# Three places instead of four in a weight ring, and a second part of a key cache kept on chip

## The chip, the cores and the metric

The kernel runs on one core of a Trainium2 chip. The core has five engines with a queue of instructions each: TensorE (PE in the profile, its weight loads PEld), VectorE (DVE), ScalarE (ACT), GpSimd (POOL) and the sync engine (SP), which here only issues DMA transfers. Sixteen DMA engines move data between HBM and SBUF, the on-chip memory of 128 partitions; matmuls write to PSUM. The metric is the device time of one execution in microseconds.

## The reference

Two sequences of one token each, width 576, run through two layers; each is an attention over a cache and a gated MLP, and both layers read the same weights and the same caches:

```python
x = A_x                                     # [2, 1, 576]
for layer in range(2):
    x = x + A(layernorm(x)); x = x + B(layernorm(x))

def A(x):                                   # 32 heads of 128, 8192 cached positions
    q = (x @ wq)                            # wq [576, 4096]
    p = softmax(einsum("bhqd,bhkd->bhqk", q, k_cache) * 128 ** -0.5)
    return einsum("bhqk,bhkd->bhqd", p, v_cache) @ wo      # wo [4096, 576]

def B(x):
    return (gelu(x @ w_gate) * (x @ w_up)) @ w_down        # inner width 4608
```

The caches are [2, 32, 8192, 128] in float32, 268 MB for the keys and as much for the values. Reading both twice is most of the work.

## The kernel before

**Items.** Each layer's attention goes through 34 items. Items 0 to 29 are pairs of heads of one sequence, whose keys are eight parts of 1024 KB (`PART`, 128 partitions x 2048 floats). Items 30 to 33 (`SINGLE[0]` to `SINGLE[3]`) are single heads, with four parts each. Layer 0 takes the items in order, layer 1 backwards, so that what layer 0 used last is used first in layer 1 and can stay on chip: the keys of items 32 and 33 (`KEYS_HELD`) and the values of items 31, 32 and 33 (`VALUES_HELD`). Of the keys of item 31, the fourth part is kept as well, copied by ScalarE into a tile of PSUM (`kept`, line 636) and copied back in layer 1 (line 679).

**An item.** VectorE multiplies a part by the query (line 644; where an item's keys stay, into one of two product buffers instead of in place), GpSimd adds the two halves (line 661), and VectorE sums the rest to the scores (line 664, `add_up`). In the first items of layer 1, GpSimd (line 648) and ScalarE (line 654) take over some rows. Then the softmax on ScalarE (lines 713 and 721), and TensorE multiplies by the values (line 762). `add_up` frees the part of the keys, `values` the part of the values.

**The arena.** One tile, `space`, holds caches and weights. Its addresses are given out while the program is written: 6 slots of four parts from address 0, and a ring of places of 2304 floats (`PLACE`, 1152 KB over all partitions) from `RING` = 5 slots on, so that the sixth slot (slot 5) and the ring share their space. With four places, the arena has 50,176 floats. Each transfer is a function in one list, `queue`, and `pump` runs the head of the list as soon as its space is free; `done(key)` frees a space and pumps. So transfers are issued on the sync queue strictly in the order of the list, and a transfer whose space is taken holds up all behind it. The wait on the chip is for the last instruction that used the space.

**The ring's users, in the order of the list.** While the held items fill the slots, all other traffic goes through the ring: at the end of attention 0 two places are taken by the product buffers (`products`, line 279: places 2 and 3) and the eight groups of wo begin in the others. The list reads: keys of item 33, values of items 31 and 32, two groups of wo, two parts of the values of item 33 (into a slot), two groups of wo, two more parts of these values, four groups of wo. Each group is one use of the ring (line 296). Then the MLP of layer 0: 18 pieces of w_gate and w_up in two halves, most as two transfers (lines 248 and 258), and nine of w_down (line 271). Then nine pieces of wq for layer 1 (lines 227 and 238), and, as the last users, parts 0, 1 and 2 of the keys of item 31 and part 0 of item 30's (line 165). All later parts go into slots that held items leave. Slot 5 is next used by the first half of the keys of item 28, when the ring's last users are through. From item 27 on the kernel is back to pairs of slots. The rest of the weights, for the end of layer 1, are put wherever there is room in the whole arena (`fit`, line 107).

**Consumers of the ring.** wo is multiplied in line 812, w_gate and w_up in line 951, w_down in line 1004, wq in line 549. Between layer parts stand a norm and, in the MLP, the activation, both short chains over VectorE, TensorE, GpSimd and ScalarE. Small matmuls without use (line 526) stand between the pieces.

Of the kernel before, what the change touches and what calls it, by code (L numbers as in the profile page):

```python
# [36 lines left out]
PART = JC * DH  # L37
SLOT = 4 * PART
NSLOT = 6
PLACE = DF // 2  # L40
NPLACE = 4
RING = 5 * SLOT
END = RING + NPLACE * PLACE
HELD = 5


# [17 lines left out]
SINGLE = range(PAIRS, N)  # L64
# [3 lines left out]
class Arena:  # L68
# [32 lines left out]
    def ring(self, key, n):  # L101

        at = self.take(key, RING + self.turn % NPLACE * PLACE, n)
        self.turn += at is not None
        return at

    def fit(self, key, n, lo=0):

        for at in [self.at, lo] + sorted(end for _, end in self.live.values()):
            if lo <= at and at + n <= END and self.take(key, at, n) is not None:  # L110
                self.at = at + n
# [11 lines left out]
def decode_layers(ctx, tc, x_in, kc, vc, wq, wo, wg, wu, wd, out):  # L123
    nc = tc.nc
# [7 lines left out]

    space = consts.tile([P, END], F32, name="space")

# [10 lines left out]
    arena = Arena()  # L145
    queue, ready, places = [], {}, {}
# [9 lines left out]
    def part_at(at, n):  # L156
        return space[:, at:at + n]

    def part(at):
        return part_at(at, PART).rearrange("p (j d) -> p j d", d=DH)  # L160
# [6 lines left out]
    def cache(key, src, n, slots=None, pieces=None):  # L167

        parts = ITEMS[n].parts

        def make():
            at = arena.pair(key) if slots is None else arena.slots(key, slots, parts)
            if at is None:
                return False
            lo = 0
            for m in pieces or (parts,):
                load(at[lo], n, src, lo, lo + m)
                lo += m
            ready[key] = dict(enumerate(map(part, at)))
            places[key] = at  # L180
            return True

        queue.append(make)

    def half(key, src, n, k, slot):

        def make():
            at = arena.slots(key, (slot,), 4, k)
            if at is None:
                return False  # L190
            load(at[0], n, src, k, k + 4)
            ready.setdefault(key, {}).update((k + i, part(a)) for i, a in enumerate(at))
            return True

        queue.append(make)

    def one(key, src, n, k, where):

        def make():
            at = arena.ring((key, k), PART) if where is None else arena.take((key, k), places[where[0]][where[1]], PART)  # L200
            if at is None:
                return False
            load(at, n, src, k, k + 1)
            ready.setdefault(key, {})[k] = part(at)
            return True

        queue.append(make)
# [13 lines left out]
    def half_rows(key, w, us, first):  # L221

        width = w.shape[1] // 2
        rows = w.rearrange("r (s w) -> (r s) w", w=width).rearrange("(p u) w -> p u w", p=P)

        def transfers(t):
            nc.sync.dma_start(t.rearrange("p (u w) -> p u w", w=width), rows[:, us[0]:us[-1] + 1, :])

        weights(key, len(us) * width, first, transfers)

    def of_half(h, k):

        width = wq.shape[1] // 2
        rows = wq.rearrange("r (s w) -> (r s) w", w=width).rearrange("(p u) w -> p u w", p=P)

        def transfers(t):
            for e in range(2):
                nc.sync.dma_start(t[e::2, :], rows[e::2, 2 * k + (h + e) % 2, :])

        weights(("wq", 1, h, k), width, None, transfers)  # L240
# [38 lines left out]
    def products():  # L279

        def make():
            at = [RING + k * PLACE for k in (2, 3)]
            if not all(arena.clear(a, PLACE) for a in at):
                return False
            ready["products"] = [part(arena.take(("products", k), at[k], PART)) for k in range(2)]
            return True

        queue.append(make)

    def out_rows(layer, g):  # L290

        rows = wo[g * GH * DH:(g + 1) * GH * DH, :].rearrange("(p i) c -> p (i c)", i=GH)
        cut = 3 * D if layer == 0 and g == groups(layer)[-1] else GH * D

        def transfers(t):
            nc.sync.dma_start(t[:, :cut], rows[:, :cut])
            if cut < GH * D:
                nc.sync.dma_start(t[:, cut:], rows[:, cut:])

        weights(("wo", layer, g), GH * D, whole_at[layer], transfers)  # L300
# [16 lines left out]
    def groups(layer):  # L317
        return range(H // GH)[::1 - 2 * layer]

    def name(kind, layer, n):  # L320

        return kind, 1 if n in (KEYS_HELD if kind == "k" else VALUES_HELD) else layer, n

    def plan_first():
# [6 lines left out]
        for us in three:  # L331
            half_rows(("wq", 0, us[0]), wq, us, END - NU * H * DH // 2)
        last = PAIRS - 1
# [28 lines left out]
    def plan_second():  # L362

        for k in range(4):
            of_half(1, k)
        half_rows(("wq", 1, NU - 1), wq, single[-1], None)
        for k in range(4):
            of_half(0, k)
        last = PAIRS - 1
        k63, v63, k62, v62 = ("k", 1, SINGLE[3]), ("v", 1, SINGLE[3]), ("k", 1, SINGLE[2]), ("v", 1, SINGLE[2])  # L370

        for k in range(3):
            one(("k", 1, SINGLE[1]), kc, SINGLE[1], k, None)
        for k in range(4):
            one(("k", 1, SINGLE[0]), kc, SINGLE[0], k, (k63, k - 1) if k else None)

        one(("k", 1, last), kc, last, 0, (k63, 3))
        turns = iter(range(1, 5)), iter(range(4))
        for kind in "vvvvkkkk":
            if kind == "k":  # L380
                k = next(turns[0])
                one(("k", 1, last), kc, last, k, (k62, k - 1))
            else:
                k = next(turns[1])
                one(("v", 1, SINGLE[0]), vc, SINGLE[0], k, (v63, k))
        for k in range(5, 8):
            one(("k", 1, last), kc, last, k, (v62, k - 5))
        half(("k", 1, last - 1), kc, last - 1, 0, 5)
        half(("k", 1, last - 1), kc, last - 1, 4, 4)
        half(("v", 1, last), vc, last, 0, 0)  # L390
        half(("v", 1, last), vc, last, 4, 1)
        for n in range(last - 2, -1, -1):
            cache(("k", 1, n), kc, n)
            cache(("v", 1, n + 1), vc, n + 1)
        cache(("v", 1, 0), vc, 0, None, (4, 2, 1, 1))
        for g in groups(1):
            out_rows(1, g)
# [16 lines left out]
    plan_first()  # L414
    plan_mlp(0)
    plan_second()
    plan_mlp(1)
    pump()
# [59 lines left out]
    kept = psum1.tile([P, JC, DH], F32, name="kept")  # L478
# [62 lines left out]
    def attention(layer):  # L541
# [55 lines left out]
        def waited(n):  # L597

            return layer == 1 and n in seq[:5]
# [21 lines left out]
        def keys(n, k, m):  # L621

            key = name("k", layer, n)
            if m == 1:
                return ready[key][k]
            return part_at(arena.live[key, k][0], m * PART).rearrange("p (j d) -> p j d", d=DH)
# [3 lines left out]
        def multiply(n, k, m):  # L630

            if k == 0:
                S[n] = work.tile([P, SK * 2 // P], F32, name="S")
            u = t = keys(n, k, m)
            if n == SINGLE[1] and k == 3 and layer == 0:
                nc.scalar.copy(kept, t)
            if layer == 0 and n in KEYS_HELD:
                u = ready["products"][k % 2]
            every = m * JC
            rows = 12 if waited(n) else every  # L640
            q = qs[:, n % 2, :]
            if rows < JC and k == 0:
                nc.scalar.copy(q, qb[n])
            nc.vector.tensor_tensor(  # L644
                out=u[:, :rows, :], in0=t[:, :rows, :], in1=qb[n].unsqueeze(1).to_broadcast([P, rows, DH]), op=ALU.mult
            )
            if rows < JC:
                nc.gpsimd.tensor_tensor(
                    out=u[:, rows:, :], in0=t[:, rows:, :], in1=q.unsqueeze(1).to_broadcast([P, JC - rows, DH]),
                    op=ALU.mult,  # L650
                )
            r = own_rows(n, k, m)
            for j in range(r, every):
                nc.scalar.activation(  # L654
                    u[:, j, :], u[:, j, :], AF.Copy, accum_out=S[n][:, k * JC + j:k * JC + j + 1]
                )
            if at_once(n, k):
                prod[n, k] = u[:, :r, :]
                return
            half = prod[n, k] = u[:, :r, :DH // 2]  # L660
            nc.gpsimd.tensor_tensor(out=half, in0=half, in1=u[:, :r, DH // 2:], op=ALU.add)  # L661
# [230 lines left out]
        n, p = seq[-1], seq[-2]  # L892
# [154 lines left out]
```

## Time and profile before

| | |
|---|---|
| median of 3 runs | 2686.63 us (2686.57 to 2686.77) |
| profiled execution | 2686.79 us, span from first to last instruction 2685.0 us |
| bytes moved | 1154.30 MB, mean 430 GB/s |
| VectorE busy | 1806.0 us (67%) |
| GpSimd busy | 1161.8 us (43%) |
| TensorE busy | 914.4 us (34%) |
| ScalarE busy | 163.7 us (6%) |

A line of the instructions in order of time has the start in us, the time in us, the engine, the line of the kernel, the operation, output <- input, the shape and the number of instructions merged, and in brackets the idle time of the engine before it and what ended that. SPq is the sync queue, where the time runs from the first issue of a merged group to the last. A table of stretches has the stretch, its length, the busy time of PE, PEld, DVE, ACT and POOL with the number of instructions, the granted clock of TensorE, the mean busy share of the 16 DMA engines (packets are counted where they start, so a short stretch can be over 1) and GB/s. In a list of waits, a line has the waiting engine, what it waited for, the total in us, how often, and the longest. In the list of queues, a line has the packets, the megabytes and the share of 16 engines' time.

### The profile page before, as it was taken

What the parts mean: (1) busy time and instruction counts of PE and PEld (TensorE: products, weight loads), DVE (VectorE), ACT (ScalarE), POOL (GpSimd) and SP (SyncE); (2) the same over time, 40 slices, a digit from 0 to 9 for tenths busy, and PEclk for the clock granted to TensorE, in tenths of its full rate; (3) what the DMA queues carried; (4) which work ended last, traced back from release to release, by engine and by line L of the source; (5) the groups of instructions that cost most, each with busy time, mean ns of one, the idle gap of its engine ahead of it and who ended that gap; (6) DMA issues with size and microseconds to landing.
All of it is one profiled execution on the core that took longest, in us unless ns stands there. A gap on an engine that the chain in (4) does not pass through costs nothing. (4 is left out here: it accounts for less than half of the span.)

```text
span 2685.0 us, 17174 instructions
## 1 busy us (share of the span) xinstructions
PE 914.4 (34%) x7150; PEld 305.4 (11%) x7150; DVE 1806.0 (67%) x874; ACT 163.7 (6%) x786; POOL 1161.8 (43%) x261
## 2 busy tenths in 40 slices
PE   1323332332233233334663333233223323332356
PEld 0100010010001000111221101001000100010022
DVE  4876687677667766867037877667766776776640
ACT  0000000000000000000026000000000000000000
POOL 2543454354445444544028455445444543454420
PEclk7656666665666566566986665666566656656678
DMA  9999999999999999999999999999999999999998
GB/s 422 436 436 426 437 432 434 433 434 432 433 431 435 436 428 433 436 428 425 414 418 434 431 431 436 431 434 434 437 428 434 434 435 431 431 434 435 433 421 375
DMA packets 33950, 1154.30 MB, mean 430 GB/s; under 512 B 4152, under 2 KB 4176, under 8 KB 5968
## 3 DMA queue, kind: packets, MB, share of 16 engines
q1 hardware_dynamic: 33832, 1153.19, 99.8%
q8 instruction: 56, 0.92, 0.1%
q14 instruction: 22, 0.18, 0.0%
q10 hardware_dynamic: 40, 0.01, 0.0%
HBM read 1153.18 MB, written 0.00 MB: 429 GB/s over the span
## 5 line engine op out<-in xcount | busy, mean ns | idle before, releaser
L661 POOL TENSOR_TENSOR space<-space 128x3072 f32<-128x3072 f32 (+3 forms) x221 | 1128.6, 5107 | 1263.3 <-DVE space L644 1202.5
L644 DVE TENSOR_TENSOR space<-space,bank 128x6144 f32<-128x6144 f32 (+3 forms) x223 | 1112.7, 4991 | 560.2 <-DMA space<-in_A_k_cache_dram 496.8
L762 PE MATMUL acc<-space,prz 128*8 128x512 f32 x4096 | 594.6, 744 | 199.4 <-DMA space<-in_A_v_cache_dram 195.5
L664 DVE TENSOR_REDUCE S<-space 128x48 f32<-128x3072 f32 (+3 forms) x223 | 569.3, 2553 | 89.9 <-POOL space L661 89.6
L592 PE MATMUL bank<-qsb,pick 4*64 4x128 f32 (+1 forms) x256 | 46.3, 436 | 863.1 <-DVE space L644 853.1
L762 PEld LDWEIGHTS acc<-space,prz 128*8 128x8 f32 x4096 | 119.1, 104 | 616.3 <-issue 410.6
L784 PE MATMUL bank<-of,osb 128*32 128x2 f32 x512 | 40.9, 202 | 324.4 <-DVE osb L777 324.4
L713 ACT ACTIVATE nbs<-bank 128x2 f32<-128x2 f32 (+1 forms) x68 | 11.6, 171 | 1848.2 <-PE bank L698 1801.8
L592 PEld LDWEIGHTS bank<-qsb,pick 4*64 4x64 f32 (+1 forms) x256 | 20.7, 202 | 882.5 <-DVE space L644 863.2
L517 POOL TENSOR_TENSOR rstd<-ve,mhalf 128x1 f32<-128x1 f32 x4 | 2.2, 550 | 168.8 <-DVE ve L515 168.8
L690 PE MATMUL bank<-ident,m 128*1 128x128 f32 x68 | 19.5, 286 | 160.7 <-DVE m L688 160.5
L784 PEld LDWEIGHTS bank<-of,osb 128*32 128x32 f32 x512 | 35.9, 154 | 331.7 <-DVE osb L777 330.5
L978 DVE STREAM_TRANSPOSE o<-o 128x288 f32<-128x288 f32 x4 | 2.8, 691 | 94.5 <-ACT o L976 94.5
L729 PE MATMUL bank<-sums,unit 128*128 128x2 f32 x120 | 35.2, 363 | 87.0 <-ACT prz L721 87.0
L776 DVE TENSOR_TENSOR acc<-acc,diag 128x512 f32<-128x512 f32 x64 | 43.5, 680 | 22.0 <-PE acc L762 22.0
L721 ACT ACTIVATE prz<-S,nbs 64x128 f32<-64x128 f32 (+1 forms) x128 | 50.7, 396 | 17.3 <-POOL prz L711 14.4
L803 ACT ACTIVATE oT<-bank,rinv 32x8 f32<-32x8 f32 x110 | 28.5, 259 | 381.5 <-PE bank L784 380.8
L654 ACT ACTIVATE space<-space 128x128 f32<-128x128 f32 x164 | 48.3, 296 | 23.6 <-DVE space L644 21.7
L698 PE MATMUL bank<-m,unit 1*128 1x2 f32 (+1 forms) x136 | 39.0, 354 | 25.3 <-DVE m L696 25.3
L777 DVE TENSOR_REDUCE osb<-acc 128x128 f32<-128x512 f32 x64 | 44.3, 691 | 2.2
L521 DVE TENSOR_TENSOR x<-bank,x 128x144 f32<-128x144 f32 x4 | 1.2, 308 | 64.1 <-PE bank L1004 40.4
L729 PEld LDWEIGHTS bank<-sums,unit 128*128 128x128 f32 x120 | 30.1, 311 | 92.2 <-ACT prz L721 92.2
(73 smaller groups left out, 427.6 us busy)
## 6 DMA issues: line engine op xcount, KB each, us to landing
space<-in_A_v_cache_dram SPq DMA_DIRECT2D x8, 4096.0 KB
space<-in_A_k_cache_dram SPq DMA_DIRECT2D x6, 4096.0 KB
space<-in_A_wo_dram SPq DMA_DIRECT2D x15, 1152.0 KB
space<-in_A_k_cache_dram SPq DMA_DIRECT2D x15, 1024.0 KB
space<-in_B_w_down_dram SPq DMA_DIRECT2D x9, 1152.0 KB
space<-in_B_w_gate_dram SPq DMA_DIRECT2D x3, 3456.0 KB
space<-in_A_v_cache_dram SPq DMA_DIRECT2D x10, 1024.0 KB
space<-in_A_wq_dram SPq DMA_DIRECT2D x3, 3072.0 KB
```

The costliest lines, as they stand in the source:

```text
L592: nc.tensor.matmul(qb[n][to, :], pick[32 * c:32 * c + 4, r:r + 1].to_broadcast([4, P // it.heads]), qsb[32 * c:32 * c + 4, (h % 4) * DH:(h ...
L644: nc.vector.tensor_tensor(out=u[:, :rows, :], in0=t[:, :rows, :], in1=qb[n].unsqueeze(1).to_broadcast([P, rows, DH]), op=ALU.mult)
L654: nc.scalar.activation(u[:, j, :], u[:, j, :], AF.Copy, accum_out=S[n][:, k * JC + j:k * JC + j + 1])
L661: nc.gpsimd.tensor_tensor(out=half, in0=half, in1=u[:, :r, DH // 2:], op=ALU.add)
L664: nc.vector.tensor_reduce(out=S[n][:, k * JC:k * JC + own_rows(n, k, m)], in_=prod.pop((n, k)), axis=AX.X, op=ALU.add)
L698: nc.tensor.matmul(mT[n][:, :heads], ones[0:1, :], m1[:, :heads], start=True, stop=True)
L721: nc.scalar.activation(pr[at, lo:].rearrange("p (g e) -> p g e", e=4)[:, 0:it.rows // 2:2, :], s[at, :it.rows].rearrange("p (g r) -> p g r ...
L729: nc.tensor.matmul(tot[n][:, :ITEMS[n].heads], ones, rs.pop(n), start=True, stop=True)
L762: nc.tensor.matmul(accumulator(n)[32 * c:32 * c + 8, :], pr[:, at:at + 8], t[g // 4][:, g % 4 * 4:g % 4 * 4 + 4, :].rearrange("p j d -> p ...
L776: nc.vector.tensor_tensor(out=q, in0=q, in1=diag.unsqueeze(2).to_broadcast([P, 4, DH]), op=ALU.mult)
L777: nc.vector.tensor_reduce(out=t, in_=q.rearrange("p r d -> p d r"), axis=AX.X, op=ALU.add)
L784: nc.tensor.matmul(po[lo:lo + 32, i, :], t[:, i::GH], of, start=True, stop=True)
```

## The change

The ring has three places. In the space of the fourth lies a new area of one part, `STAY`, and part 2 of the keys of item 31 is copied there by ScalarE in layer 0 and used from there in layer 1, where it is no longer read from HBM. The arena ends 256 floats earlier. Both copies of item 31, the one to `STAY` and the one to `kept`, are now issued ahead of the item's first multiplication rather than before its fourth. The product buffers lie in places 1 and 2, so that one place, not two, is free for wo beside them.

```diff
 PLACE = DF // 2
-NPLACE = 4
+NPLACE = 3
 RING = 5 * SLOT
-END = RING + NPLACE * PLACE
+STAY = RING + NPLACE * PLACE
+END = STAY + PART
...
     def products():
...
-            at = [RING + k * PLACE for k in (2, 3)]
+            at = [RING + k * PLACE for k in (1, 2)]
...
-        for k in range(3):
+        for k in range(2):
             one(("k", 1, SINGLE[1]), kc, SINGLE[1], k, None)
...
             u = t = keys(n, k, m)
-            if n == SINGLE[1] and k == 3 and layer == 0:
-                nc.scalar.copy(kept, t)
+            if n == SINGLE[1] and k == 0 and layer == 0:
+
+                ready["k", 1, n] = {2: part(arena.take((("k", 1, n), 2), STAY, PART))}
+                nc.scalar.copy(ready["k", 1, n][2], keys(n, 2, 1))
+                nc.scalar.copy(kept, keys(n, 3, 1))
```

## The prediction

> **What bounds the kernel now.** I read the head of the page first, then the whole span's waits, then a table of stretches around the change, and last the instructions of the sync queue, TensorE and VectorE in order of time.
>
> ```profile
> span 2685.0 us, 17174 instructions
> DMA  9999999999999999999999999999999999999998
> HBM read 1153.18 MB, written 0.00 MB: 429 GB/s over the span
> ...
> DVE space L644 <- DMA space<-in_A_k_cache_dram: 496.8, 57, 24.0
> ...
> 2680.45 1.14 PE L1004 MATMUL bank<-space,hT 128*4 128x144 f32 x24 [0.48 <-DMA space<-in_B_w_down_dram]
> ```
>
> The 16 DMA engines are busy in every slice, VectorE waits 496.8 us for keys, and the last matmuls wait for the last weights 4.5 us before the end. So the bound is the stream of bytes from HBM. A step that shortens the stream pays in full; a step that makes the stream run dry costs in full; compute counts only where it decides when the next transfer may be issued. The span is 2685.0 us, the profiled execution 2686.79 us, and the median 2686.63 us: the sum below is a difference, and I put it on the median.
>
> The change acts between the end of layer 0's attention and the start of layer 1's:
>
> ```profile
> 1258.00:1266.00 8.00, 7.42 (x85) 2.37 (x73) 2.31 (x6) 0.61 (x3) 1.95 (x2) 0.92 1.01 421
> 1284.00:1300.00 16.00, 11.61 (x168) 5.47 (x166) 2.62 (x11) 0.00 (x0) 0.55 (x1) 0.89 1.01 404
> 1384.00:1408.00 24.00, 11.33 (x69) 3.02 (x67) 16.22 (x15) 11.08 (x73) 10.89 (x10) 0.72 1.01 423
> 1408.00:1433.00 25.00, 9.91 (x52) 3.65 (x48) 19.74 (x23) 19.75 (x120) 21.73 (x17) 0.67 1.01 420
> ```
>
> The last two columns are the busy share of the DMA engines and GB/s. The share is 1.01 throughout: with four places the stream has no hole here. The question is whether three leave one.
>
> **The part that goes.** One piece of the key cache of item 31, 1024 KB, is no longer read a second time. 1,048,576 bytes at 420 to 423 GB/s are 2.48 to 2.50 us: **-2.49 us**. One issue less on the sync queue (0.33 us, the row of 1432.83 below) is worth nothing, since transfers are issued well ahead of the stream.
>
> **The copies.** ScalarE copies two parts of item 31 instead of one, both when that item's keys have landed.
>
> ```profile
> 1210.12 2.29 DVE L644 TENSOR_TENSOR space<-space,bank 128x2048 f32<-128x2048 f32 x1 [13.11 <-DMA space<-in_A_k_cache_dram]
> 1216.85 0.17 ACT L713 ACTIVATE nbs<-bank 128x1 f32<-128x1 f32 x1 [30.29 <-PE bank L698]
> 1217.23 2.26 DVE L644 TENSOR_TENSOR space<-space,bank 128x2048 f32<-128x2048 f32 x1
> 1218.94 1.86 ACT L636 COPY kept<-space 128x2048 f32<-128x2048 f32 x1
> ```
>
> Two copies of 1.86 us from 1210.1 end by 1213.9. ScalarE has been idle for 30.29 us and is next wanted at 1216.85; VectorE overwrites the third part at 1217.23 and the fourth after it. Both are over by then: 0 us, hidden by ScalarE's idle time (without it, at most 1.86 us, on a compute chain with the stream running beside it). In layer 1 the third part is read from its new address by the same instruction.
>
> **Addresses.** The arena is 256 floats shorter. I walked the allocator's order for the weights of layer 1 by hand: the highest end is 49,536 of now 49,920, so each keeps its address and its moment: 0 us.
>
> **The ring.** Each transfer through the ring now waits for the piece three before it, not four.
>
> ```profile
> 1257.22 1.21 DVE L664 TENSOR_REDUCE S<-space 128x16 f32<-128x1024 f32 x1
> 1233.48 0.86 SPq L296 DMA_DIRECT2D space<-in_A_wo_dram  x2
> 1234.39 0.90 SPq L165 DMA_DIRECT2D space<-in_A_v_cache_dram  x2
> 1258.46 2.95 SPq L296 DMA_DIRECT2D space<-in_A_wo_dram  x2
> 1265.54 10.60 SPq L296 DMA_DIRECT2D space<-in_A_wo_dram  x4
> 1272.04 1.17 PE L812 MATMUL bank<-space,oT 128*4 128x144 f32 x32 [1.30 <-DMA space<-in_A_wo_dram]
> 1274.84 1.16 PE L812 MATMUL bank<-space,oT 128*4 128x144 f32 x32 [1.22 <-DMA space<-in_A_wo_dram]
> 1277.32 1.04 PE L762 MATMUL acc<-space,prz 128*8 128x512 f32 x8 [0.91 <-DMA space<-in_A_v_cache_dram]
> ```
>
> First point. With two places under the products, only one group of wo goes ahead of them. The second, issued before at about 1233.9, waits until the first product buffer is free, at 1258.46 (the reduction ends at 1258.43). Behind it in the sync queue stand two pieces of values (1234.39), so three transfers are held back some 24 us. When is the stream through with the first wo? The PE rows give landings: a wo group takes 1274.84 - 1272.04 = 2.80 us, a piece of values 1277.32 - 1274.84 = 2.48. The third wo landed at 1272.04; taking off itself, two pieces of values and the second wo (2.80 + 2.48 + 2.48 + 2.80 = 10.56) gives 1261.48. What does a transfer need from issue to landing besides its bytes? The one that meets an empty queue is the output:
>
> ```profile
> 2682.00 0.64 SPq L1019 DMA_DIRECT2D out_dram<-x  x1
> 2683.50:2684.00 0.50, 0.00 (x0) 0.00 (x0) 0.00 (x0) 0.00 (x0) 0.00 (x0) 1.00 0.02 5
> 2684.00:2685.00 1.00, 0.00 (x0) 0.00 (x0) 0.00 (x0) 0.00 (x0) 0.00 (x0) 1.00 0.00 0
> ```
>
> Its bytes move until between 1.5 and 2.0 us after the issue: I take **2.0 us** as start-up. It is a small transfer in a quiet chip, so for a loaded queue I keep a far upper end: the piece of wq issued at 1372.97 (below) had until 1377.98, the landing before it, and the stream shows no hole, so 5.0 us is all that the rows exclude. 1258.46 + 2.0 = 1260.46, which is 1.0 us before 1261.48: covered, barely. The following groups are freed by matmuls as before (1265.54 onward), with more to spare.
>
> Then the even flow, the norms, and the return to keys:
>
> ```profile
> 1296.75 1.11 SPq L258 DMA_DIRECT2D space<-in_B_w_gate_dram  x2
> 1299.48 1.16 PE L951 MATMUL acc<-space,xt 128*8 128x288 f32 x16 [0.35 <-DMA space<-in_B_w_gate_dram]
> 1348.43 1.16 PE L1004 MATMUL bank<-space,hT 128*4 128x144 f32 x32 [0.95 <-DMA space<-in_B_w_down_dram]
> 1351.07 1.16 PE L1004 MATMUL bank<-space,hT 128*4 128x144 f32 x32 [0.63 <-DMA space<-in_B_w_down_dram]
> 1353.87 1.16 PE L1004 MATMUL bank<-space,hT 128*4 128x144 f32 x32 [0.79 <-DMA space<-in_B_w_down_dram]
> 1372.97 0.33 SPq L227 DMA_DIRECT2D space<-in_A_wq_dram  x1
> 1375.51 1.04 PE L549 MATMUL acc<-space,xt 128*4 128x512 f32 x8 [1.03 <-DMA space<-in_A_wq_dram]
> 1377.98 1.04 PE L549 MATMUL acc<-space,xt 128*4 128x512 f32 x8 [1.03 <-DMA space<-in_A_wq_dram]
> 1390.38 1.04 PE L549 MATMUL acc<-space,xt 128*4 128x512 f32 x8 [1.04 <-DMA space<-in_A_wq_dram]
> ```
>
> Even flow: a piece lands every 2.7 us (1348.43, 1351.07, 1353.87) and its matmuls take 1.16. The place is refilled behind two pieces under way, 5.4 us, and asks for 1.16 + 2.0 = 3.2: 2.2 us to spare, 0 us lost. It would lose only from a start-up of 5.4 - 1.2 = 4.2 us.
>
> Second point, the norm of the MLP. The first pieces of w_gate are held until the norm is done; the place of the first is free at 1296.75. Its next user was the middle piece, now it is the fourth w_gate. That must be in the stream when the third has landed, at 1299.48. 1296.75 + 2.0 = 1298.75: 0.7 us to spare. Third point, the norm of layer 1: the first piece of wq frees its place at 1372.97, now needed when the third has landed, at 1375.51; 1374.97, 0.5 us to spare.
>
> Fourth point. From 1390.38 on the stream carries key and value pieces of 1024 KB up to the first half of item 28's keys, whose slot 5 overlaps the ring and the new place; that half waits for item 30's first piece, a reduction:
>
> ```profile
> 1383.99 17.09 SPq L165 DMA_DIRECT2D space<-in_A_k_cache_dram  x8
> 1405.07 3.50 SPq L165 DMA_DIRECT2D space<-in_A_v_cache_dram  x4
> 1408.67 33.83 SPq L165 DMA_DIRECT2D space<-in_A_k_cache_dram  x9
> 1432.03 0.73 DVE L664 TENSOR_REDUCE S<-space 128x9 f32<-128x576 f32 x1
> 1432.83 0.33 SPq L165 DMA_DIRECT2D space<-in_A_k_cache_dram  x1
> ```
>
> Of the nine, two are item 28's halves, so 8 + 4 + 7 = 19 pieces; at 2.49 us they end at 1390.38 + 47.3 = 1437.7. With 18 they end at 1435.2. The reduction at 1432.03 stands in a chain of VectorE, GpSimd and ScalarE on data that landed long before, so it does not come earlier: 1432.83 + 2.0 = 1434.8, and 0.4 us are left. The 2.49 us pass this point. Behind it item pairs wait for the stream (the 496.8 us above), so the gain stays to the end.
>
> **What the thin places cost.** A transfer is over when the slowest of 16 engines is through, and engines also fetch code:
>
> ```profile
> q8 instruction: 9, 0.15, 0.4%
> space<-in_A_k_cache_dram SPq DMA_DIRECT2D x8, 1024.0 KB
> ```
>
> This is 1258 to 1408. Nine fetches take 0.4% of 16 x 150 us, 1.07 us each, on one engine. With much queued, the other engines run ahead meanwhile and an engine that is hit catches none of them up, but one that was ahead hides its hit. At each thin point engines that are ahead stop until the rest are within 0.4 to 1.0 us, and the next fetch on one of them is not hidden. No row shows this loss; below, it is 0; above, one fetch after each of the first three points, 3.2 us. I take one fetch, **+1.07**, as each point still leaves 0.5 to 1.0 us of cover.
>
> Sum: -2.49 + 0 + 0 + 0 + 1.07 = -1.4 us; 2686.63 - 1.4 = 2685.2 us.
>
> **The rivals.**
> - Fetches stay hidden. The stream keeps its full gain: 2686.63 - 2.49 = 2684.1. For it: all points are covered at 2.0 us and the share is 1.01 despite nine fetches. Against it: covers under 1.07 us at every point. The Trainium skill (Runtime: NRT & Kernel Launch, section Instruction fetch mechanics) says that code comes in 16 KiB blocks whose fetching is mostly hidden, and by that this rival would hold; the trace agrees on the size (0.15 MB in nine).
> - The gain is given back: three fetches are paid, -2.49 + 3.2 = +0.7, or start-up is 3 us, which overdraws the second to fourth points by 0.3, 0.5 and 0.6: 2687.3, both together 2688.7.
> - The saved read does not matter: a start-up of 4.9 us at slot 5 eats the 2.49 by itself, as 1432.83 does not move: 2686.6.
> - Slower: the ring runs dry at every turn. Price: start-up less 4.2 us, at some 33 turns; it outweighs 2.49 from 4.3 us, and reaches 0.2% (5.4 us) from 4.45. At 5.0 us it is 33 x 0.8 - 2.5 = +24, 2710. Against it: the output's 1.5 to 2.0 us.
>
> **How the numbers follow.** About 0.2%, 5.4 us, is what a measurement tells from no change. Likeliest (2685.2, own range 2684.6 to 2686.2) 0.47; fetches hidden 0.22; given back 0.20; lost at slot 5 0.05; ring dry 0.05; a gain over 5.4 us, for which I see no source, 0.01. All but the last two lie within 0.2%: same 0.94, slower 0.05, faster 0.01. The range goes from the full gain (2684.1, less 0.2 for the spread of the rates, 2683.9) to both losses of the third case, 2688.7, and leaves out some 1 in 10.
>
> **What would show it.** Right: 1.05 MB fewer read; the second wo issued at about 1258.5 with two pieces of values right behind; DMA share near 1.0 in each stretch from 1258 to 1433; the last piece before item 28's keys through some 1.5 to 2.5 us earlier, and from there every row earlier by the same. Wrong: a stretch with a share under 0.95, matmuls of w_down landing more than 2.8 us apart, or item 28's first half issued later than 1433.

## The result, and the profile after

The median of 13 runs is 2693.48 us (2690.08 to 2696.7), against 2686.63 us (2686.46 to 2687.08) in 13 runs of the kernel before: 6.9 us slower, a ratio of 1.0026 with an interval of 1.0019 to 1.0034. The forecast, 2685.2 us in a range to 2688.7, missed by 8.3 us and had the wrong sign. The profiled execution took 2696.57 us, near the top of the 13, so its trace shows 9.8 us where the median lost 6.9; sizes below are read from medians, places from the trace.

The head of the page of the changed kernel, the line of its waits for keys, and the last matmuls in order of time:

```profile
span 2694.8 us, 17166 instructions
HBM read 1152.13 MB, written 0.00 MB: 428 GB/s over the span
...
GB/s 420 434 436 433 434 431 433 434 429 435 432 432 432 434 434 434 435 425 413 388 395 418 439 432 430 434 434 434 432 430 434 431 436 433 432 433 432 433 422 369
...
DVE space L648 <- DMA space<-in_A_k_cache_dram: 498.2, 57, 23.9
...
2690.28 1.15 PE L1008 MATMUL bank<-space,hT 128*4 128x144 f32 x24 [0.49 <-DMA space<-in_B_w_down_dram]
```

The 1.05 MB are indeed no longer read (1153.18 before). Three slices in the middle, where the ring works, fall to 413, 388 and 395 GB/s. VectorE's wait for keys is what it was (496.8), and the end still waits for the last weights, only later. So the bound is the same stream; it runs slower in one place. The stretches of that place, before the change and after it (columns as in the prediction: granted clock, DMA share and GB/s stand last):

```profile
1300.00:1336.00 36.00, 19.71 (x226) 6.61 (x219) 1.85 (x7) 0.97 (x3) 0.00 (x0) 0.98 1.01 415
1336.00:1360.00 24.00, 17.13 (x262) 8.10 (x261) 1.84 (x7) 0.97 (x3) 0.00 (x0) 0.96 1.01 422
1360.00:1392.00 32.00, 21.19 (x224) 7.02 (x216) 6.14 (x12) 2.67 (x13) 3.06 (x3) 1.00 1.01 414
1392.00:1420.00 28.00, 8.85 (x44) 3.33 (x44) 23.59 (x24) 18.54 (x121) 20.70 (x16) 0.63 1.01 421
```

```profile
1258.00:1266.00 8.00, 6.44 (x77) 2.26 (x69) 3.29 (x7) 0.61 (x3) 2.27 (x2) 1.00 0.87 344
1284.00:1300.00 16.00, 11.75 (x186) 5.95 (x178) 2.65 (x12) 0.00 (x0) 0.55 (x1) 0.89 0.99 390
1300.00:1336.00 36.00, 20.91 (x213) 6.91 (x213) 1.85 (x7) 0.97 (x3) 0.00 (x0) 0.91 0.99 387
1336.00:1360.00 24.00, 15.22 (x200) 6.26 (x196) 1.85 (x7) 0.97 (x3) 0.00 (x0) 0.93 0.99 397
1360.00:1392.00 32.00, 21.48 (x277) 8.55 (x270) 4.49 (x11) 1.21 (x4) 2.40 (x3) 0.96 0.99 380
1392.00:1420.00 28.00, 13.73 (x75) 3.57 (x70) 18.83 (x16) 14.25 (x94) 13.64 (x11) 0.74 0.99 387
```

Only the first of these stretches has a hole in the share (0.87). In all others the share still reads 0.99 while GB/s are 14 to 34 below before. A share near 1 with fewer bytes means that packets take longer, and the list of queues for 1258 to 1425 says so (before, then after; columns: packets, MB, share of 16 engines):

```profile
q1 hardware_dynamic: 10205, 69.45, 100.7%
q8 instruction: 9, 0.15, 0.4%
```

```profile
q1 hardware_dynamic: 9572, 64.91, 98.1%
q8 instruction: 9, 0.15, 0.3%
```

Per packet, 1.007 x 167 us x 16 / 10205 = 0.264 us before and 0.981 x 167 x 16 / 9572 = 0.274 us after. Among the packets of the usual size, 41 of 8,699 took over 0.25 us longer than usual before, and 210 of 8,141 after. Over 9,572 packets on 16 engines, 0.010 us more per packet is 6 us of the stream; the 2.6% of share that is missing is another 4.3 us. The code fetches (queue 8) are nine in both kernels.

**Where the lateness arises.** Each transfer leaves one record of landing per DMA engine. A matmul can start at the last of the sixteen (the second w_down has its last record at 1354.20, and its matmuls start at 1354.25); the first shows how far the engines are apart. For some transfers of the changed kernel, worked out from these records: the lead (from the issue to the last landing of the transfer before), the step from that landing to its own last one, the same step in the kernel before, how much later than before it lands, and the spread from first to last engine, after and before. All in us.

```
                     issue    lead   step  (before)   late   spread (before)
first wo            1233.80  25.19   2.77   2.79      0.29    5.28   4.81
second wo           1258.77   2.99   2.79   2.79      0.29    1.04   4.81
values 33, part 1   1259.62   7.43   2.99   2.47      0.83    1.55   4.77
fourth w_gate       1298.43   1.99   2.28   1.39      1.96    0.72   3.90
third w_up, 2nd     1309.14   5.50   2.83   1.39      4.19    2.44   2.18
first w_down        1342.83   4.20   3.18   2.78      4.87    1.36   3.53
second w_down       1345.33   4.88   3.99   3.05      5.81    2.35   3.79
fourth w_down       1351.57   5.42   2.79   2.79      5.96    2.38   3.66
fourth wq           1379.17   2.63   2.04   1.24      7.23    1.34   3.62
last wq             1392.24   3.43   1.78   1.24      8.45    1.67   2.44
keys 31, part 1     1396.90   4.60   2.45   2.48      8.74    1.16   2.44
keys 30, part 0     1399.94   4.01   2.49   (left out) 6.25
values 30, part 0   1413.53   2.84   4.52   2.48      8.29
keys 28, first half 1441.27   4.99   9.72   9.70      8.87
```

There is no single hole. Of the 101 transfers that both kernels issue here, 19 cost 0.2 us or more than before, 12.1 together; the others step as before or make up a little, and one makes up 0.9. The 19 are of two kinds. Ten, 6.8 us together, were issued with leads of only 2.0 to 4.5 us, and the trace has no code fetch of queue 8 beside them. The other nine, 5.2 us together, have a code fetch beside them: one engine of the sixteen spends 0.9 to 1.1 us on it between the first landing of the transfer before and the transfer's own last one. Among these nine are all seven losses with a lead above 4.6 us (4.7 to 12.3), although only 27 of the 101 transfers have a fetch beside them. The transfer that makes up 0.9 is one where a fetch, at 1328.00, held up the kernel before as well.

At "keys 30" the unread part pays its 2.5 us, and at "values 30" 2.0 of them are gone. From item 28 on both kernels run in step, 8.9 us apart, up to a piece of the last w_down, which takes 4.11 us instead of 3.18 and makes it 9.8.

### The profile page after: what moved, and what is told of

Read it like the earlier page. It is cut to its first block, busy times and chain, and to the rows that moved or that the text cites. A ratio compares the mean times of both kernels' runs of the same rounds, so it can differ in the third digit from the quotient of the medians.

```text
span 2694.8 us, 17166 instructions
## 1 busy us (share of the span) xinstructions
PE 924.3 (34%) x7150; PEld 307.3 (11%) x7150; DVE 1806.0 (67%) x874; ACT 165.5 (6%) x787; POOL 1161.8 (43%) x261
```

## The experiments

Theory A: a transfer that goes through the ring needs more than 2 us of lead, since the engines that run ahead of the slowest empty first; three places do not give that lead. Theory B (mine of the prediction): 2 us are enough, and something else costs, the hold at the products or the code fetches. For the saved read: it is worth 2.5 us wherever the stream is the bound, or it is lost where the compute sets the issue times.

**The two halves of the change.** The first kernel has the three places, and reads the part again into `STAY`:

```diff
             one(("k", 1, SINGLE[1]), kc, SINGLE[1], k, None)
+        places["stay"] = [STAY]
+        one(("k", 1, SINGLE[1]), kc, SINGLE[1], 2, ("stay", 0))
...
-                ready["k", 1, n] = {2: part(arena.take((("k", 1, n), 2), STAY, PART))}
-                nc.scalar.copy(ready["k", 1, n][2], keys(n, 2, 1))
```

> The ring of three alone: item 31's third part is read again, straight into the new area, and is not copied there. Theory A (look-ahead): with two pieces under way instead of three, DMA engines that run ahead empty at nearly every turn, and the packets with which an empty engine starts again take longer; the stream falls behind by 5 to 9 us, and the saved read was given back where the first values of item 30 are issued, since that moment hangs on the compute, which is as late. So about the changed kernel: +5 to +9 over before, 2692 to 2696. Theory B (the copies or the new area cost the time): no copy to it here, so 2686 to 2688. Theory C (the saved read pays in full inside the changed kernel): changed kernel + 2.5, about 2696.

Measured: 2695.69 us (2694.95 to 2697.71) against 2686.74, ratio 1.0034 [1.0022, 1.0047]: +9.0 us. The second kernel has four places and drops the read alone (what lies in its place is multiplied instead):

```diff
-                load(at, n, src, k, k + 1)
+            if read:
+                load(at, n, src, k, k + 1)
...
-            one(("k", 1, SINGLE[1]), kc, SINGLE[1], k, None)
+            one(("k", 1, SINGLE[1]), kc, SINGLE[1], k, None, k < 2)
```

> The saved read alone: four places as before, the place for item 31's third part is taken but not filled (the multiplication uses what lies there, so this part of the scores is left out). As predicted for the term: -2.49 us, 2684.1. Theory A (look-ahead): the transfers behind come 2.49 us sooner to the values of item 30, issued 5.0 us ahead before and 2.5 now, so engines empty there: -2 to -0.5, 2684.6 to 2686.1. If the read is hidden anyway: 2686.6.

Measured: 2687.38 us (2686.55 to 2688.24), ratio 1.0002 [0.9993, 1.0011]: no gain at all. So the ring is the whole loss, and the saved read earns nothing even beside an intact ring. Where it goes, the stretches and the sync queue of this kernel show:

```profile
1393.00:1405.00 12.00, 3.48 (x17) 1.41 (x21) 9.80 (x10) 6.53 (x42) 6.51 (x5) 0.61 0.96 371
1405.00:1413.00 8.00, 3.49 (x30) 0.84 (x22) 7.38 (x8) 7.28 (x48) 7.77 (x6) 0.93 0.98 352
1413.00:1433.00 20.00, 9.00 (x46) 3.09 (x46) 15.36 (x18) 15.29 (x91) 16.74 (x14) 0.66 1.01 424
1405.22 3.66 SPq L165 DMA_DIRECT2D space<-in_A_v_cache_dram  x4
```

The first keys of item 30 land 2.36 us earlier than before. The values of item 30 are issued at 1405.22, against 1405.07 before: they wait until TensorE has used item 33's values in the same space, and that does not come earlier. The stream is through with the keys ahead of them 2.0 us sooner, the lead is 2.91 us instead of 5.05, and the transfer lands 4.38 us after the previous one instead of 2.48. The read is saved, and the time is spent waiting for a place. Another 0.9 us goes a little later, at a piece of item 29's keys with 12.2 us of lead and a code fetch beside it.

**How much lead a transfer needs.** Three kernels with four places differ only in where the product buffers lie, which sets when the second wo may be issued: 6.5, 3.0 and 0.3 us ahead of the last landing of the first (the last was planned as 0.4).

```diff
# 6.5 us: a third buffer in place 1, free one part earlier
-            at = [RING + k * PLACE for k in (2, 3)]
+            at = [RING + k * PLACE for k in (2, 3, 1)]
...
# 3.0 us
+            at = [RING + k * PLACE for k in (1, 3)]
# 0.3 us
+            at = [RING + k * PLACE for k in (3, 1)]
```

> Kernel before with four places; only the second group of wo is held back (with the two pieces of values behind it), by a third product buffer that is used once. It is issued some 6.5 us before the stream is through with the first group. As predicted (2.0 us suffice): 0. Theory A (an engine that has run ahead empties, and a transfer needs 4 to 5 us of lead on the slowest engine): 0 to +0.4.

> Kernel before with four places; only the second group of wo is held back, by a product buffer in its place, until 3.0 us before the stream is through with the first group, the lead that it has in the changed kernel. As predicted: 0. Theory A: +0.5 to +1.5.

> Kernel before with four places; only the second group of wo is held back, by the other product buffer in its place, until 0.4 us before the stream is through with the first group. As predicted: +1.6 (2.0 less 0.4). Theory A: +2.5 to +4.

Measured: 2686.68 us (ratio 1.0000 [0.9991, 1.0009]), 2687.63 (1.0004 [0.9995, 1.0013]) and 2690.14 (1.0012 [1.0003, 1.0021]) against 2686.66: 0, +1.0 and +3.5 us. Between the last two the cost grows by 2.5 us over 2.65 us of lead; a straight line through them ends near 4 us at no lead, which is an estimate. The middle point alone is not resolved from zero. The stretch 1258 to 1266 in the three, in that order:

```profile
1258.00:1266.00 8.00, 7.36 (x81) 2.38 (x73) 2.17 (x6) 0.61 (x3) 1.67 (x2) 0.92 1.01 424
```

```profile
1258.00:1266.00 8.00, 7.42 (x85) 2.37 (x73) 2.34 (x6) 0.61 (x3) 1.97 (x2) 0.92 0.89 354
```

```profile
1258.00:1266.00 8.00, 7.41 (x85) 2.38 (x73) 2.33 (x6) 0.61 (x3) 1.95 (x2) 0.92 0.61 224
```

The landing records say what happens. In all three, the first engine is through with the first wo at 1256.4 to 1256.7 and the last at 1261.4 to 1261.5, 4.8 to 5.0 us apart. With 3.0 us of lead the issue (1258.48) comes 2.0 us after the first engine has run empty. The first landing of the second wo is at 1263.08, 4.60 after the issue; less the time of its bytes (2.79) that is a start-up of 1.8 us, and 1.9 in the other two. The slowest engine is hardly late (0.4 us), but the spread falls from 5.0 to 1.6 us: the engines ahead have lost their head start. With 6.5 us of lead (issue 1254.92, 1.8 us before the first engine is through), spread and time stay. At 0.3 us the slowest engine waits too. There hardly anything else is under way, and the packets show what the start-up is made of: the issue is at 1261.08, the first packet starts at 1262.05, and the first sixteen packets take 0.44 to 1.35 us each, where the usual one of this size takes 0.35. So some of the long packets are those with which an empty engine starts again.

**The hold taken out of the changed kernel.** The products go to a slot that is free then, and wo has all three places:

```diff
-            at = [RING + k * PLACE for k in (1, 2)]
-            if not all(arena.clear(a, PLACE) for a in at):
+            at = [SLOT + k * PART for k in (2, 3)]
+            if not all(arena.clear(a, PART) for a in at):
```

> Changed kernel, but the two product buffers lie in the second half of slot 1 (the third and fourth part of item 33's values come there later), so that all three places are free for wo and its second group isn't held. Theory A: the part of the loss that comes before the MLP goes, 0.5 to 1.5 us less than the changed kernel, 2692 to 2693; the turns of MLP and wq cost as before. As predicted (that hold costs nothing): same as the changed kernel, 2693.5.

Measured: 2693.54 us (2690.99 to 2695.7) against 2686.66, ratio 1.0025 [1.0014, 1.0035]: by the median the same as with the hold, so the 0.5 to 1.5 us that theory A expected did not come back. The stretch 1258 to 1266 is whole again, and the loss stands in the next ones:

```profile
1258.00:1266.00 8.00, 7.03 (x81) 2.38 (x73) 2.48 (x6) 0.61 (x3) 1.73 (x2) 0.95 1.01 422
1284.00:1300.00 16.00, 11.03 (x154) 5.05 (x156) 2.61 (x11) 0.00 (x0) 0.56 (x1) 0.89 0.95 362
1300.00:1336.00 36.00, 20.42 (x213) 6.37 (x202) 1.84 (x7) 0.97 (x3) 0.00 (x0) 0.91 1.00 392
```

What the hold took in the way of head start, the last group of wo and the first w_gate take now (issued at 1283.44 and 1286.46, with leads of 4.55 and 4.36 us; the spread falls from 4.6 to 1.5 us). At the fourth w_gate this profile is 1.0 us late and that of the changed kernel 2.0, but 1 us is not told apart in medians of kernels whose runs vary by 5 to 7 us. The holes seem to replace each other more than they add up; that is argued, not shown.

**Three places for a part of the time.** Four places, but only three of them are used by the MLP of layer 0 (turns 8 to 34, the edit shown), and in a second kernel by wq and the two pieces of keys behind it (turns 35 to 45):

```diff
-        at = self.take(key, RING + self.turn % NPLACE * PLACE, n)
+        place = (self.turn - 8) % 3 if 8 <= self.turn < 35 else self.turn % NPLACE
+        at = self.take(key, RING + place * PLACE, n)
```

> Kernel before, but the 27 pieces of the MLP of layer 0 go round in three of the four places; wo, wq and the keys as before, nothing saved. Theory A: +2 to +5 over before, the stream late by 0.2 to 0.5 us at many turns. As predicted (even flow has 2.2 us to spare, the norm 0.7): 0 to +0.5. Theory B: 0.

> Kernel before, but the nine pieces of wq and the first keys behind them go round in three places; wo and the MLP as before, nothing saved. Theory A: +1.5 to +3 over before, as the profile of the changed kernel shows the stream falling 2.3 us further behind from wq's first piece to the keys. As predicted (0.5 us to spare at the norm): 0 to +0.5. Theory B: 0.

Measured: 2691.81 us (2688.82 to 2693.62), ratio 1.0017 [1.0008, 1.0026], +5.1 us for the MLP; 2690.35 us (2688.85 to 2692.33), ratio 1.0014 [1.0005, 1.0023], +3.6 us for wq, both against 2686.74. With the hold's 1.0 that makes 9.7, where the ring alone cost 9.0; each of these sizes is known to 2 or 3 us only, so this says no more than that no large part is missing. The MLP was then halved, with three places for w_down alone (turns 26 to 34) and for the second half of gate and up alone (turns 17 to 25):

```diff
+        t, a, b = self.turn, 26, 35
+        cycle = lambda t: (a + 1 + (t - a) % 3) % 4
+        later = [a % 4, cycle(b - 3), cycle(b - 2), cycle(b - 1)]
+        place = t % 4 if t < a else cycle(t) if t < b else later[(t - b) % 4]
```

> Kernel before, but only the nine pieces of w_down go round in three places: the even flow alone, with no norm in it. As predicted (2.2 us to spare): 0. Theory A: the lead on the slowest engine is 4.2 to 4.3 us there in the changed kernel, the edge of what the holds showed (0 at 6.5 us, 1.0 at 3.0 us): 0 to +1.

> Kernel before, but only the nine pieces of the second half of w_gate and w_up go round in three places: even flow of pieces that come as two transfers each, with no norm in it. As predicted: 0. Theory A: leads of 3.3 to 4.3 us at the turns, where engines that are ahead empty: +1 to +3.

Measured: 2688.29 us (2686.8 to 2691.0), ratio 1.0006 [0.9997, 1.0015], and 2688.42 us (2686.53 to 2691.24), ratio 1.0006 [0.9997, 1.0014], against 2686.7: +1.6 and +1.7 us, neither resolved from zero by its interval. They are a third of the MLP's loss each, as their turns would have it; that they cost something is also said by the single runs, which reach 2691, where 33 runs of the kernel before reached 2688.4. The long packets go with the places: of the 49 packets over 0.25 us longer than usual in the run with w_down alone (1258 to 1425), 23 start between 1338 and 1354, where the kernel before has one.

**What the saved byte is worth elsewhere.** Four places, and the last part of item 10's keys in layer 1 is not read (what lies in its space is multiplied instead), far behind the ring:

```diff
-            for m in pieces or (parts,):
+            for m in (parts - 1,) if key == ("k", 1, 10) else pieces or (parts,):
```

> Kernel before, but the last 1024 KB of the keys of item 10 are not read in layer 1 (what lies there is multiplied, so this part of the scores is left out): a read saved where the stream runs far ahead of the compute. If a saved read pays only where the next issues don't hang on the compute: -2.49, 2684.2. If the price of a read was wrong everywhere: about 0.

Measured: 2684.11 us (2683.94 to 2685.33) against 2686.7, ratio 0.9990 [0.9981, 0.9999]: -2.6 us, the full price of 1024 KB. So the price in the prediction was right, and the place decides.

**The read dropped, with warmer matmuls in front.** In the kernel with the read dropped alone, TensorE's granted clock is 0.61 in the stretch from 1393 to 1405, ahead of and into the matmuls with the values of item 33. Sixteen products without use are put there, so that the first of these values are done sooner:

```diff
             if first:
+                idle_products(16)
                 query(seq[i + 1])
```

> The saved read alone in four places, as in that experiment (a part of the scores left out), and 16 idle matmuls ahead of layer 1's first values, so that TensorE gets a higher clock for them and the places of item 33's values come free sooner. If the saved read is lost because the values of item 30 are issued only when TensorE is through with item 33's: part comes back, 0.5 to 1.5 us less than the saved read alone. If it is lost elsewhere: same as the saved read alone, 2687.4.

Measured: 2687.08 us (2685.86 to 2687.96), ratio 1.0000 [0.9992, 1.0009]: no change that is resolved, where 0.5 to 1.5 us were expected (0.3 under the run without them). The granted clock from 1393 to 1405 is now 0.95. The values of item 30 are now issued at 1404.08, 1.1 us earlier, with a lead of 4.16, and nothing is lost there:

```profile
1404.08 4.60 SPq L165 DMA_DIRECT2D space<-in_A_v_cache_dram  x4
1405.00:1413.00 8.00, 3.60 (x22) 0.81 (x14) 7.08 (x7) 7.37 (x49) 8.00 (x7) 0.71 1.01 426
1433.00:1460.00 27.00, 14.12 (x83) 4.23 (x83) 23.92 (x26) 20.77 (x135) 23.00 (x19) 0.69 1.01 423
```

352 GB/s have become 426, and the stream runs 1.9 us ahead of the kernel before. Of these, 0.7 us go at a piece of item 29's keys with a code fetch beside it (lead 10.73 us). At the second half of item 28's keys the same happens as at the values: their place is freed by the compute of an earlier item, the lead is 3.23 us, the step 11.33 us instead of 9.73, and behind it the stream is 0.45 us late (423 GB/s from 1433 to 1460, where the kernel before has 434). Between 1391 and 1460 the compute sets when places come free, and a stream that gets ahead waits at the next one.

## Why the prediction was wrong

- **"Its bytes move until between 1.5 and 2.0 us after the issue: I take 2.0 us as start-up."** As a start-up this was right: 1.8 to 2.0 us, measured at the second wo under load. What it was set against was wrong, and this is the step that failed. I took the end of the previous transfer from the rows of matmuls, which start at the landing of the last of 16 engines. An engine runs empty at its own end, and the first is 2.0 to 4.8 us ahead of the last in the kernel before. To leave nobody idle, the issue must come 2 us before the first engine's end, 4 to 7 before the last one's. Every point of the sum compared 2.0 us with the wrong end.
- **First point, the second wo held to 1258.46, "covered, barely".** The order was as described. In the sync queue of the changed kernel the second wo is the last issue of the first row, at 1258.77, and the values stand right behind it:

```profile
1233.80 25.30 SPq L297 DMA_DIRECT2D space<-in_A_wo_dram  x2
1259.15 0.90 SPq L166 DMA_DIRECT2D space<-in_A_v_cache_dram  x2
```

  Alone, that hold costs +1.0 us by its median, not 0, though its interval does not exclude 0; taking it out of the changed kernel shows no saving in the medians.
- **The even flow, "2.2 us to spare, 0 us lost".** The spare was nought. In w_down the first two pieces lose 0.4 and 0.9 us with leads of 4.20 and 4.88 us, the second with a code fetch beside it, while the next five step as before (2.8 us) with leads of 4.3 to 5.8: most pieces get through, and nothing is left for a slow packet. The matmuls of the second to fourth piece:

```profile
1354.25 1.16 PE L1008 MATMUL bank<-space,hT 128*4 128x144 f32 x32 [1.89 <-DMA space<-in_B_w_down_dram]
1357.04 1.16 PE L1008 MATMUL bank<-space,hT 128*4 128x144 f32 x32 [0.79 <-DMA space<-in_B_w_down_dram]
1359.83 1.16 PE L1008 MATMUL bank<-space,hT 128*4 128x144 f32 x32 [0.78 <-DMA space<-in_B_w_down_dram]
```

  The first of these rows is 5.8 us behind the same group before (1348.43). The rival "the ring runs dry at every turn" had this mechanism, and with a start-up of 4.48 us its formula, 33 x 0.28 - 2.5 = +6.7, would come close to the +6.9 measured. But the trace does not show 33 equal losses: 19 of 101 transfers lose, by 0.2 to 2.0 us each, nine of them beside a code fetch, so that closeness is luck. I gave this rival 0.05, on the strength of the one row of the output in a quiet chip.
- **Second and third point, the norms: "0.7 us to spare" and "0.5 us to spare".** Right places, wrong sign: the fourth w_gate has 1.99 us of lead and loses 0.89, the fourth wq 2.63 and loses 0.80. A start-up of 2.9 to 3.4 us for the slowest engine fits these two.
- **"What the thin places cost ... I take one fetch, +1.07."** The records agree with the mechanism, that engines ahead stop at a thin point and what hits one of them afterwards is no longer hidden: the spread, 2.0 to 4.8 us before, is mostly 1 to 2.5 us, and nine transfers with a code fetch beside them lose 5.2 us. The size was wrong: less the 0.9 us made up at the fetch at 1328.00, the fetches cost 4.3 us in the profiled execution, against 1.07 in the sum and 3.2 at its upper end. I let one fetch be felt behind each of three points at most, but the spread stays small to the end of the ring, and eight of the nine fetches between 1258 and 1425 fall beside a loss. The profiles of the ring alone and of the products in a slot agree: there too, every loss of 0.2 us or more with a lead above 4.6 us has a code fetch beside it. The rival that the fetches stay hidden fails by the same numbers. To this come the data packets that take longer, 210 instead of 41; no run takes the fetches or the long packets away, so the split rests on the records alone.
- **"-2.49 us" for the read.** The price is right (-2.6 where the stream leads). That **"the gain stays to the end"** is wrong. The third rival, "the saved read does not matter", was right in its mechanism and missed the place: it is lost at the values of item 30, issued at 1413.53 in the first row below, and not at slot 5, the last issue of the second row (1441.27), where the step is as before. I checked only the last point at which a place comes free, not each of them.

```profile
1413.53 4.75 SPq L166 DMA_DIRECT2D space<-in_A_v_cache_dram  x4
1418.38 23.22 SPq L166 DMA_DIRECT2D space<-in_A_k_cache_dram  x8
```

- **"The gain is given back":** of its two cases, only three fetches give 2687.3. A start-up of 3 us alone would be -2.49 + 0.3 + 0.5 + 0.6 = -1.1, or 2685.5. The forecast does not rest on it.
- **The copies and the addresses, 0 us:** nothing in the runs speaks against it. The ring alone, without the second copy, is no faster than the changed kernel.

What the runs do not settle: the changed kernel lost 6.9 us, the ring alone 9.0, and the read alone earned nothing. The 2.1 us between the first two may be the read, which in a late stream could keep a part, or spread: kernels with three places vary by 3 to 7 us from run to run, the one before by 0.6 to 2. Nor is it settled why packets take longer where engines have run empty. A kernel with the third part kept and four places was not run; by the run with the read dropped it would gain nothing, and no kernel here that computes everything beats the kernel before.

## What to carry to other kernels

A ring that feeds a bandwidth-bound stream has to be refilled before the first DMA engine has run empty, not before the last has landed; take the cover from the first landing record of the previous transfer, add the start-up, and count what is left as protection against code fetches and single slow packets, not as spare. A busy share near 1 does not show a healthy stream; compare GB/s in the same stretch. Before crediting a saved read, go through every later point at which the compute frees a place and see whether the transfer there would be issued earlier too.

## What the runs showed of the hardware

- The sixteen engines land their parts of a transfer 2.0 to 4.8 us apart in this stretch of the kernel before, and the gap closes to about 1 us when the queue runs short once (1.04 us after the hold at 1258.77).
- A code fetch takes one engine 0.9 to 1.1 us. With the engines 4.8 us apart, the fetches at 1267.69 and 1278.29 of the kernel before cost the stream nothing; with them 1 to 2.5 us apart, transfers beside a fetch took up to 1.4 us longer.
- The first engine is through with a transfer that met an empty engine 1.8 to 2.0 us after the issue plus the time of the bytes. The Trainium skill (DMA: Bandwidth & Descriptors, section Anatomy of one DMA) gives a fixed cost of about 2.0 us for transfers issued by GpSimd; here the sync engine issues, and by the first engine the trace agrees. For the last engine it does not: 2.9 us at the fourth w_gate, 3.4 at the fourth wq, 4.9 at the values of item 30 (leads of 1.99, 2.63 and 2.84, losses of 0.89, 0.80 and 2.04).
- The busy share counts an engine as busy in packets that take longer: 0.99 at 380 to 397 GB/s, 1.01 at 414 to 422.
